# Attention in chunks: pairs of batch entries, each head in a column tile of its own

## The chip, the cores and the metric

One core of a Trainium2 chip runs the whole program. The metric is the device time of one execution in microseconds (us), from the first to the last instruction. TensorE (PE) multiplies matrices; its weight loads stand apart in the profile (PEld). VectorE (DVE), ScalarE (ACT) and GpSimd (POOL) work on elements, and SyncE (SP) issues nearly all DMAs. Matmul results land in PSUM, from where DVE or ACT must move them ("evacuate") to SBUF.

## The reference, cut to what matters

Three stages follow each other. First a recurrence over 768 steps for each of 4 batch entries and 8 heads, with a state of 40x40:

```
for t in range(S):
    y[:, :, t] = einsum('bhd,bhde->bhe', rt, state)
    Sa = einsum('bhde,bhe->bhd', state, at)
    state = state * wt[:, :, None, :] - einsum('bhd,bhe->bhde', Sa, bt)
    state = state + einsum('bhd,bhe->bhde', vt, kt)
```

Its output, as 3072 tokens of 320 values, goes through a mixture of 8 experts (one expert for each token, two layers of 320x1024 and 1024x320), and then through `(a * b) @ w_out` with `a = x @ w_a` and `b = x @ w_b` (1536 wide). The change touches the first stage alone.

## The kernel before, in words

**Chunks.** The recurrence is computed in 12 chunks of 64 steps. Inside a chunk it becomes matrix products: grams of the scaled keys and gates (`gram`), the inverse of a triangular 64x64 matrix (`invert` on DVE and POOL for the 32x32 blocks, `merge` on PE for the block that couples them), then the chain that carries the state, and the outputs. `cum` and `prod` scale the operands, which go to DRAM and come back spread over the partitions (`fetch`, `rfetch`, `spread`).

**Pairs.** Two heads of 64 steps share the 128 partitions: p = 0 in partitions 0 to 63, p = 1 in 64 to 127. A chunk has 16 pairs k, in four groups of four (q = 0 to 3), and the code calls such a group b. Before, a pair is two heads of one batch entry and b is the batch entry.

**The chain of a group** (`chain`, lines 341 to 400) has five parts, C0 to C4. C0 (lines 347 to 358) makes x: for each q one fp16 matmul of `a3` (128 columns of weights, both heads) with the state S of both heads (80 columns), and two float32 matmuls of 64x64 weights with 40 columns, one for each head. The fp16 product gives four blocks of 64x40, of which the two that join a head with its own state are used; so the rows of p = 0 are read at other columns than those of p = 1, and the evacuation is two ACT instructions. C1 (lines 360 to 367) makes u, 64x64 weights and 40 columns, a quadrant of the array for each head. C2 (lines 371 to 385) makes the new state: for each q one fp16 matmul with `sel` (128 columns of weights, 80 streamed) and two float32 matmuls of 128x40 weights, evacuated by two DVE instructions that scale by the decay. C3 and C4 (lines 387 to 399) spread the state over the partitions, and transpose it.

**The outputs of a group** (`outs`, lines 402 to 439): O0 splits and transposes u; O1 makes nf; O2 (lines 422 to 432) makes y: for each q one fp16 matmul of `r3` with the transposed state and one float32 matmul of `nf` (128 columns of weights, both heads) with `z` of both heads (80 columns), evacuated by two DVE instructions. O3 is the gate of the next stage (`gate1`, matmuls at lines 554 and 560).

**float32.** Each float32 matmul of the attention appears in the trace as two loads and two matmuls, that is, two passes: C0 has 16 float32 matmul instructions for its 8 products.

**The order of the work.** `PLAN` (line 479) gives each part of a chunk a place in time, in units of one chunk, and `run` emits the parts sorted by it; the framework then orders the instructions of each engine (line 1038). Each engine takes its queue in order. The preparation of later chunks is emitted between the chains of earlier ones. `warm` (line 336) puts fp16 matmuls of 256 or 512 columns, whose result is overwritten, ahead of most PSUM tiles. The buffers that the change touches: `GT` (scales of y, 3), `QF` (tiles of v and u, 5, one for each group), `Q3`, `P1b`, and `pm`, the PSUM tile of `merge`.

Of the kernel before, what the change touches and what calls it, by code (L numbers as in the profile page):

```python
# [23 lines left out]
def sub(ap, off, dims):  # L24
    """AP on the same tensor: keeps the partition dim of ap, free dims replaced."""
    return bass.AP(tensor=ap.tensor, offset=ap.offset+off, ap=[list(ap.ap[0])]+[list(d) for d in dims])

def host_layout(inp, NC=12):
    f=np.float32
    d={}  # L30
    ct=np.zeros((12,128,5,12,64),f)
    ct[:,:,0]=1.0
    for n,nm in enumerate('wakbr'):
        x=np.asarray(inp[nm]).reshape(4,4,2,12,64,40)       # b q p c t e
        x=x.transpose(3,2,0,1,5,4).reshape(12,2,16,40,64)   # c p k e t
# [15 lines left out]
class Attn:  # L51
    CE=staticmethod(lambda nc: nc.gpsimd)
    PP=(1, 2)
    NP=10      # columns of the inverse (of 16 a partition) that the vector engine computes
    def __init__(s, ctx, tc, ct, vt, x, NC, moe=None):
        s.moe=moe
        s.tc=tc; s.nc=tc.nc; s.ct=ct; s.vt=vt; s.x=x; s.NC=NC
        nc=tc.nc
        mk=lambda n,b,**k: ctx.enter_context(tc.tile_pool(name=n,bufs=b,**k))
        # what is free early lies at the ends, where the next stage's first tiles go  # L60
# [3 lines left out]
        s.ch={}      # per chunk tiles  # L64
# [17 lines left out]
    def setup2(s):  # L82
        nc=s.nc; c=s.c
        z0=c.tile([128,1],F32,name="zz"); nc.gpsimd.memset(z0,0.0)
        s.Z=[c.tile([128,16*104+24],F32,name=f"Z{i}") for i in range(NZ)]     # k p e
        s.TT=[c.tile([128,16,64],F32,name=f"TT{i}") for i in range(2)]
        s.T11=c.tile([128,16,32],F32,name="T11")
        s.P1b=[c.tile([128,4,32],F32,name=f"P1b{i}") for i in range(2)]
        s.DT=[c.tile([128,18],F32,name=f"DT{i}") for i in range(4)]
        s.Q3=[c.tile([128,4,2,128],F16,name=f"Q3{i}") for i in range(QN)]  # L90
# [13 lines left out]
    def scr(s,n,shape,dt,c):  # L104
        """DRAM that is used again: it bounds how far the preparation runs ahead"""
# [4 lines left out]
    def pmt(s,name,n):  # L110
        if n%4==0: s.pm=s.ps.tile([128,512],F32,tag="pm",name=name,bufs=1)
        return s.pm[:,128*(n%4):128*(n%4)+128]
    def tile(s,shape,dt,tag,name,bufs): return (s.pl if tag[:3]=="raw" or tag=="dl" else s.pr if tag in EARLY else s.p2 if tag in MID else s.p3 if tag in LATE else s.p).tile(shape,dt,tag=tag,name=name,bufs=bufs)
    # ---- chunk preparation in the transposed layout
# [5 lines left out]
    def cum(s,c):  # L120
# [63 lines left out]
        # y scale  # L184
# [5 lines left out]
        # decay of the carried state  # L190
# [11 lines left out]
    # ---- spread of the operands over the partitions  # L202
# [35 lines left out]
    # ---- grams and the blocks to invert  # L238
    def gram(s,c):
# [10 lines left out]
        tin=s.dr.tile([2,2,16,32,32],F32,tag="tin",name=f"tin{c}")   # blk p k s t  # L250
# [9 lines left out]
    def invert(s,c):  # L260
# [20 lines left out]
        td=s.dr.tile([2,2,16,32,32],F32,tag="td",name=f"td{c}")     # blk p k s t  # L281
# [11 lines left out]
    def merge(s,c):  # L293
# [3 lines left out]
        for b in range(4):  # L297
            k0=4*b; P1b=s.P1b[b%2]
            pp=s.pmt(f"p1{c}{b}",2*b)
            for q in range(4):  # L300
# [11 lines left out]
            for r in (0,64):  # L312
                nc.scalar.activation(TT[r:r+32,k0:k0+4,32:64],pq[r:r+32,0:128].rearrange("p (q t) -> p q t",q=4),AF.Copy)
# [11 lines left out]
    def vload(s,c):  # L325
        vr=s.tile([128,4,4,40],F32,"vr",f"vr{c}",1)
        s.nc.sync.dma_start(vr.rearrange("p b q e -> p (b q e)"),s.vt[c])
        s.ch.setdefault(c,{})['vr']=vr
    def vsplit(s,c,b):
        nc=s.nc; vr=s.ch[c]['vr'][:,b]  # L330
        Q=s.tile([128,4,2,40],F32,"Q32",f"Qf{c}{b}",QF)
# [3 lines left out]
        s.ch[c][b]=Q  # L335
    def warm(s,ps,k):
        """the array's clock halves when it streams for less than a certain share of the time: columns ahead of the tile's own"""
        n=WARM[k]
        if n: s.nc.tensor.matmul(ps[:,0:n],s.sel[:,4],s.sel[:,0:4].rearrange("p a b -> p (a b)")[:,0:n],start=True,stop=True)
    # ---- one batch entry of one chunk: the chain  # L340
    def chain(s,c,b):
# [4 lines left out]
        s3=lambda t,q: t[0:120,80*q:80*q+80]  # L346
# [18 lines left out]
        for p in (0,1):  # L365
            r=slice(64*p,64*p+64)
            nc.scalar.activation(Q[r,:,p],pu[r,0:160].rearrange("p (q e) -> p q e",q=4),AF.Copy)
        yield
        if c+1<s.NC:
            dt=s.DT[(c+1)%4]  # L370
            pS=s.pst(f"S{c}{b}","pc",2); s.warm(pS,2)
            for q in range(4):
                o=pS[:,q*80:q*80+80]
                if S: mm(o,s.sel[0:120,4],s3(S[0],q),start=True,stop=False)
                n=104*(k0+q)
                if not S: mm(o,z[:,n:n+128],Q[:,q].rearrange("r p e -> r (p e)"),start=True,stop=True)      # 24 columns more are there than used
                else:
# [23 lines left out]
    # ---- one batch entry of one chunk: the outputs  # L401
    def outs(s,c,b):
# [19 lines left out]
        py=s.pst(f"y{c}{b}","po",3); s.warm(py,4)  # L422
        for q in range(4):
# [16 lines left out]
    def step(s,c,b,g,i):  # L440
        """the i-th part of the chain (g=0) or of the outputs (g=1) of one batch entry"""
# [37 lines left out]
PLAN=dict(cum=(18,-3.456,-2.906),prod=(5,-2.906,-2.556),fetch=(3,-2.506,-2.411),gtr=(3,-0.907,-0.897),ztr=(6,-1.79,-1.011),gram=(6,-1.932,-1.922),rfetch=(1,-1.246,-1.236),invert=(64,-1.815,-1.381),tload=(1,-1.122,-1.067),merge=(9,-0.659,-0.209),vpre=(6,-0.796,-0.088),C0=(4,-0.081,-0.071),C1=(4,-0.047,0.086),C2=(4,0.191,0.462),O0=(4,0.315,0.573),C3=(4,0.462,0.734),C4=(4,0.463,0.735),O1=(4,0.586,0.858),O2=(4,0.718,0.96),O3=(2,0.96,1.028))  # L479
# [3 lines left out]
KE=3; CX=8       # blocks that are filled from the first chunks' tokens alone; these chunks  # L483
# [559 lines left out]
```

## Time and profile before

| | |
|---|---|
| median of 3 runs | 1615.24 us |
| the runs | 1615.66, 1615.24, 1597.02 us |
| profiled execution, first to last instruction | 1600.6 us |
| TensorE busy, share of the span | 1331.0 us, 83% |
| VectorE | 897.3 us, 56% |
| ScalarE | 561.6 us, 35% |
| GpSimd | 572.6 us, 36% |
| mean granted TensorE clock, share of the full 2.4 GHz | 0.802 |

The profiled execution has no time beside its span; the span lies between the lowest run and the other two. In the table's shares all three stages are mixed. The matmuls of the first chunk's chain begin around 227 us and the attention's last matmul lies at about 884 us; experts and the last stage follow. A granted clock of 0.50 is 1.2 GHz, one of 1.00 is 2.4 GHz. In a row of a timeline, the first number is the start, the second the time until the modelled end of the last instruction of the row, and "xN" the number of merged instructions; the modelled ends overlap the next row, so durations are read from start to start.

### The profile page before, as it was taken

What the parts mean: (1) busy time and instruction counts of PE and PEld (TensorE: products, weight loads), DVE (VectorE), ACT (ScalarE), POOL (GpSimd) and SP (SyncE); (2) the same over time, 40 slices, a digit from 0 to 9 for tenths busy, and PEclk for the clock granted to TensorE, in tenths of its full rate; (3) what the DMA queues carried; (4) which work ended last, traced back from release to release, by engine and by line L of the source; (5) the groups of instructions that cost most, each with busy time, mean ns of one, the idle gap of its engine ahead of it and who ended that gap; (6) DMA issues with size and microseconds to landing.
All of it is one profiled execution on the core that took longest, in us unless ns stands there. A gap on an engine that the chain in (4) does not pass through costs nothing. (4 is left out here: it accounts for less than half of the span.)

```text
span 1600.6 us, 28092 instructions
## 1 busy us (share of the span) xinstructions
PE 1331.0 (83%) x10765; PEld 1087.4 (68%) x10765; DVE 897.3 (56%) x2192; ACT 561.6 (35%) x1214; POOL 572.6 (36%) x754
## 2 busy tenths in 40 slices
PE   0211279896799999999997989899979999999998
PEld 0111268675577787777886878777856887878787
DVE  9668878566754454454524639998989212121111
ACT  4211345343353443343434224544423223132221
POOL 4535655443442112022115026664445223141221
PEclk9999976555555555555565889998989999999999
DMA  6866655544643323122133126666531101000000
GB/s 207 230 200 188 177 148 155 171 102 136 162 122 96 93 72 96 47 87 65 45 87 95 33 79 192 200 210 183 163 95 62 29 5 33 17 17 18 0 17 17
DMA packets 165284, 166.19 MB, mean 104 GB/s; under 512 B 92213, under 2 KB 130421, under 8 KB 165141
## 3 DMA queue, kind: packets, MB, share of 16 engines
q1 hardware_dynamic: 162741, 156.12, 34.1%
q0 software_dynamic: 2400, 8.20, 1.8%
q8 instruction: 86, 1.41, 0.4%
q14 instruction: 57, 0.47, 0.1%
HBM read 118.43 MB, written 45.84 MB: 103 GB/s over the span
## 5 line engine op out<-in xcount | busy, mean ns | idle before, releaser
L767 POOL TENSOR_TENSOR pL<-pr,pH 128x512 fp32r<-128x512 f32 x72 | 93.0, 1291 | 261.8 <-ACT pH L769 261.7
L786 PE MATMUL ab<-X2H,abh 128*128 128x512 f32 x432 | 172.8, 402 | 1.2 <-ACT sa L977 0.6
L276 DVE TENSOR_TENSOR mA<-tA,tl 128x120 f32<-128x120 f32 (+24 forms) x372 | 115.0, 318 | 83.9 <-DMA tl<-tin 79.3
L978 DVE TENSOR_TENSOR pr<-ab,sa 128x512 f32<-128x512 f32 x72 | 49.6, 689 | 181.4 <-ACT sa L977 181.4
L247 PE MATMUL g<-a,kb 120*128 120x64 f16 x384 | 30.6, 237 | 119.9 <-DMA r<-dr 48.4
L247 PEld LDWEIGHTS <-kb 120*128 120x128 f16 x384 | 25.6, 127 | 153.9 <-issue 132.6
L279 DVE TENSOR_TENSOR tA<-tA,mA 128x120 f32<-128x120 f32 (+24 forms) x372 | 115.2, 320 | 4.8
L426 PE MATMUL y<-Z,nf 128*128 128x80 f32 x384 | 112.6, 449 | 3.6 <-DVE nf L420 3.6
L786 PE MATMUL ab<-X2L,abh 128*128 128x512 f32 x288 | 113.0, 394 | 0.0
L426 PEld LDWEIGHTS y<-Z,nf 128*128 128x128 f32 x384 | 103.5, 333 | 6.6 <-DVE nf L420 3.9
L977 ACT ACTIVATE sa<-ab 128x512 f32<-128x512 f32 x72 | 42.9, 595 | 179.7 <-PE ab L788 179.7
L786 PE MATMUL ph<-XHb,w1h 128*128 128x256 f32 x312 | 93.4, 324 | 6.0 <-DVE hL L855 5.5
L786 PEld LDWEIGHTS ab<-X2H,abh 128*128 128x128 f32 x432 | 81.8, 190 | 21.5 <-issue 2.9
L988 PE MATMUL po<-woh,pH 128*128 128x320 f32 x288 | 93.2, 328 | 3.2 <-ACT woh L932 2.7
L109 POOL TENSOR_TENSOR Q<-Qf,Q 128x320 f16<-128x320 f32 x48 | 39.1, 814 | 154.2 <-ACT Q L407 115.7
L767 POOL TENSOR_TENSOR w1l<-wr,w1h 128x512 fp32r<-128x512 f32 x51 | 70.8, 1404 | 54.2 <-ACT w1h L809 42.0
L786 PE MATMUL ab<-X2H,abl 128*128 128x512 f32 x288 | 89.4, 391 | 0.0
L988 PE MATMUL po<-wol,pH 128*128 128x320 f32 x288 | 88.8, 312 | 0.0
L988 PE MATMUL po<-woh,pL 128*128 128x320 f32 x288 | 88.2, 312 | 0.0
L276 POOL TENSOR_TENSOR mB<-tA,tl 128x18 f32<-128x18 f32 (+7 forms) x121 | 31.0, 256 | 142.8 <-DMA tl<-tin 135.7
L769 ACT ACTIVATE pH<-pr 128x512 fp32r<-128x512 f32 x72 | 45.5, 632 | 100.8 <-DVE pr L978 68.5
L353 PE MATMUL x<-Qf,gm 64*64 64x40 f32 x768 | 77.3, 278 | 0.0
(309 smaller groups left out, 3682.2 us busy)
## 6 DMA issues: line engine op xcount, KB each, us to landing
raw<-ct SPq DMA_DIRECT2D x60, 384.0 KB
kb<-dk SPq DMA_DIRECT2D x36, 360.0 KB
wr<-moe_w SPq DMA_DIRECT2D x40, 320.0 KB
wr<-moe_w SPq DMA_DIRECT2D x40, 256.0 KB
dk<-kb SPq DMA_DIRECT2D x12, 720.0 KB
r<-dr SPq DMA_DIRECT2D x36, 180.0 KB
a<-da SPq DMA_DIRECT2D x36, 180.0 KB
tl<-tin SPq DMA_DIRECT2D x12, 512.0 KB
```

The lines of the kernel that those rows point to most:

```text
L109: def psub(s,out,a,b): s.nc.gpsimd.tensor_tensor(out=out,in0=a,in1=b,op=ALU.subtract)
L247: nc.tensor.matmul(pg[:,(q*2+p)*64:(q*2+p)*64+64], d['kb3'][0:120,k,p], d['a3'][0:120,k,64*p:64*p+64], start=True,stop=True)
L276: E.tensor_tensor(out=t,in0=sub(tA[:,lo,0:1],j,[[32,k],[0,n]]),in1=sub(tl[:,0,0:1],32*j+j+1,[[0,k],[1,n]]),op=ALU.mult)
L279: for E,t,o in ps: E.tensor_tensor(out=o,in0=o,in1=t,op=ALU.add)
L353: mm(px[64*p:64*p+64,q*80+40*p:q*80+40*p+40],gm[r,k0+q,p],Q[r,q,p],start=not S,stop=True)
L426: mm(o,nf[:,2*q:2*q+2].rearrange('p a t -> p (a t)'),sub(z[:,0:1],104*(k0+q),[[64,2],[1,40]]),start=SR is None,stop=True)
L767: def psub(s,L,a,H): s.nc.gpsimd.tensor_tensor(out=L,in0=a,in1=H,op=ALU.subtract)
L769: s.nc.scalar.activation(H,src,AF.Copy)
L786: for i,(a,b) in enumerate(l): mm(o,a,b,start=(i==0),stop=False)
L977: sa=w.tile([128,512],F32,tag="sa",name=f"sa{g}{m}"); nc.scalar.activation(sa,pp[0],AF.Copy)
L978: pr=w.tile([128,512],F32,tag="pr",name=f"pr{g}{m}"); V.tensor_tensor(out=pr,in0=pp[1],in1=sa,op=ALU.mult)
L988: nc.tensor.matmul(po,a[:,m,tk],b[:,m],start=(n==0),stop=(n==35)); n+=1
```

## The change

A pair becomes two batch entries with the same head (the host layout places them so), and a group b is half the heads of two batch entries. Then the products of each head go to the partitions of that head alone (an output at 64p), at columns 40q: each is a matmul of 64 columns of weights with 40 streamed columns, in one of two column tiles of the array, and no cross-head block is computed. In C0 an fp16 matmul with zero weights `zh` clears the PSUM tile, then all `a3` products follow, then all float32 products; in C2 two `sel` products of 160 columns come first, then all `z` products; in O2 each q has two `r3` and two `nf` products. x, the new state and y then lie at the same columns for both p, and one instruction evacuates each. `merge` works on eight pairs at a time in place of four, and the copy of v (`vsplit`) on two groups at a time, with `QF` counting tiles of two groups. `GT` goes from 3 to 2. In `PLAN`, `merge` has 5 parts in place of 9 and `vpre` 4 in place of 6, in the same stretches of time. All other changed lines are comments and docstrings.

```diff
-        x=np.asarray(inp[nm]).reshape(4,4,2,12,64,40)       # b q p c t e
-        x=x.transpose(3,2,0,1,5,4).reshape(12,2,16,40,64)   # c p k e t
+        x=np.asarray(inp[nm]).reshape(2,2,8,12,64,40)
+        x=x.transpose(3,1,0,2,5,4).reshape(12,2,16,40,64)
...
-KB,R3,A3,NZ,GT=1,3,3,4,3
-QN,QF=3,5
+KB,R3,A3,NZ,GT=1,3,3,4,2
+QN,QF=3,3
...
+        s.zh=c.tile([128,128],F16,name="zh"); nc.gpsimd.memset(s.zh,0.0)
...
-        for b in range(4):
-            k0=4*b; P1b=s.P1b[b%2]
+        for b in range(2):
+            k0=8*b; P1b=s.P1b[b%2]
...
-            nc.vector.tensor_scalar(out=Q[r,:,p],in0=vr[r],scalar1=NU,scalar2=None,op0=ALU.mult)
+            nc.vector.tensor_scalar(out=Q[r,:,p].rearrange("r b q e -> r b (q e)"),in0=vr[r,2*f:2*f+2],scalar1=NU,scalar2=None,op0=ALU.mult)
...
-        px=s.pst(f"x{c}{b}","pc",2); s.warm(px,0)
+        px=s.pst(f"x{c}{b}","pc",2)
+        o=lambda t,q,p,n=64: t[64*p:64*p+n,40*q:40*q+40]
+        if S:
+            mm(px[:,0:160],s.zh,s.sel[:,0:2].rearrange("p a b -> p (a b)")[:,0:160],start=True,stop=False)
+            for q in range(4):
+                for p in (0,1):
+                    mm(o(px,q,p),d['a3'][0:120,k0+q,64*p:64*p+64],S[0][0:120,80*q+40*p:80*q+40*p+40],start=False,stop=False)
         for q in range(4):
-            o=px[:,q*80:q*80+80]
-            if S: mm(o,d['a3'][0:120,k0+q],s3(S[0],q),start=True,stop=False)
             for p in (0,1):
                 r=slice(64-64*p,128-64*p)
-                mm(px[64*p:64*p+64,q*80+40*p:q*80+40*p+40],gm[r,k0+q,p],Q[r,q,p],start=not S,stop=True)
+                mm(o(px,q,p),gm[r,k0+q,p],Q[r,p,q],start=not S,stop=not S or q==3)
...
-        for p in (0,1):
-            r=slice(64*p,64*p+64)
-            nc.scalar.activation(X[r],px[r,0:320].rearrange("p (q a e) -> p q a e",q=4,a=2)[:,:,p],AF.Copy,scale=xs)
+        nc.scalar.activation(X,px[:,0:160].rearrange("p (q e) -> p q e",q=4),AF.Copy,scale=xs)
...
+            if S:
+                for p in (0,1):
+                    mm(pS[64*p:64*p+64,0:160],s.sel[0:120,4,64*p:64*p+64],S[0][0:120].rearrange("p (q a e) -> p a q e",q=4,a=2)[:,p],start=True,stop=False)
             for q in range(4):
-                o=pS[:,q*80:q*80+80]
-                if S: mm(o,s.sel[0:120,4],s3(S[0],q),start=True,stop=False)
...
-                    for p in (0,1): mm(o[64*p:64*p+40,40*p:40*p+40],z[:,n+64*p:n+64*p+40],Q[:,q,p],start=False,stop=True)
+                for p in (0,1):
+                    n=104*(k0+q)+64*p
+                    if S: mm(o(pS,q,p,40),z[:,n:n+40],Q[:,p,q],start=False,stop=(q==3))
+                    else: mm(o(pS,q,p),z[:,n:n+64],Q[:,p,q],start=True,stop=True)
...
         for q in range(4):
-            o=py[:,q*80:q*80+80]
-            if SR is not None: mm(o,r3[0:120,k0+q],SR[0:120,q].rearrange("p a e -> p (a e)"),start=True,stop=False)
-            mm(o,nf[:,2*q:2*q+2].rearrange('p a t -> p (a t)'),sub(z[:,0:1],104*(k0+q),[[64,2],[1,40]]),start=SR is None,stop=True)
+            if SR is not None:
+                for p in (0,1): mm(o(py,q,p),r3[0:120,k0+q,64*p:64*p+64],SR[0:120,q,p],start=True,stop=False)
+            for p in (0,1):
+                n=104*(k0+q)+64*p
+                mm(o(py,q,p),nf[:,4*p+q],z[:,n:n+40],start=SR is None,stop=True)
...
-            for p in (0,1):
-                r=slice(64*p,64*p+64)
-                V.tensor_tensor(out=tS[r],in0=pS[r,0:320].rearrange("p (q a e) -> p q a e",q=4,a=2)[:,:,p],in1=sub(dt[r,0:1],k0,[[1,4],[0,40]]),op=ALU.mult)
+            V.tensor_tensor(out=tS,in0=pS[:,0:160].rearrange("p (q e) -> p q e",q=4),in1=sub(dt[:,0:1],k0,[[1,4],[0,40]]),op=ALU.mult)
...
-        for p in (0,1):
-            r=slice(64*p,64*p+64)
-            V.scalar_tensor_tensor(out=y[h,:,p],in0=py[r,0:320].rearrange("p (q a e) -> p q a e",q=4,a=2)[:,:,p],scalar=ys,in1=d['gt'][r,k0:k0+4],op0=ALU.mult,op1=ALU.mult)
+        V.scalar_tensor_tensor(out=y[:,b%2],in0=py[:,0:160].rearrange("p (q e) -> p q e",q=4),scalar=ys,in1=d['gt'][:,k0:k0+4],op0=ALU.mult,op1=ALU.mult)
```

## Rows read from the trace of the kernel before

**Rows 1.** The page: busy time of the engines, and the granted clock in 40 slices.
```profile
PE 1331.0 (83%) x10765; PEld 1087.4 (68%) x10765; DVE 897.3 (56%) x2192; ACT 561.6 (35%) x1214; POOL 572.6 (36%) x754
...
PEclk9999976555555555555565889998989999999999
```

**Rows 2.** Windows: length, busy time (instructions) of PE, PEld, DVE, ACT, POOL; clock; DMA.
```profile
335.00:416.00 81.00, 61.04 (x644) 47.99 (x643) 57.20 (x168) 31.08 (x72) 40.80 (x60) 0.54 0.48 128
...
598.00:656.00 58.00, 54.18 (x603) 43.66 (x600) 26.45 (x98) 23.20 (x63) 11.96 (x33) 0.56 0.26 78
...
227.00:884.00 657.00, 598.25 (x6393) 488.62 (x6391) 351.41 (x1123) 274.36 (x678) 204.09 (x388) 0.56 0.37 102
```

**Rows 3.** Waits of PE, 227 to 884 us: total us, times, longest.
```profile
PE g L247 <- DMA a<-da: 9.9, 3, 3.9
PE y L339 <- DVE nf L420: 8.2, 2, 6.4
```

**Rows 4.** Timeline of PE: n of one group, then y of another.
```profile
561.22 0.61 PE L418 MATMUL n<-r,uv 120*128 120x64 f16 x8
561.64 0.40 PE L339 MATMUL y<-sel 128*128 128x256 f16 x1
561.83 0.27 PE L425 MATMUL y<-SR,r 120*128 120x80 f16 x1
561.90 0.69 PE L426 MATMUL y<-Z,nf 128*128 128x80 f32 x2
...
564.07 0.42 PE L339 MATMUL y<-sel 128*128 128x256 f16 x1
```

**Rows 5.** Timeline of PE: the new state (C2) of one group.
```profile
579.25 0.27 PE L374 MATMUL S<-S,sel 120*128 120x80 f16 x1
579.46 0.36 PE L378 MATMUL S<-Qf,Z 128*40 128x40 f32 x4
579.75 0.25 PE L374 MATMUL S<-S,sel 120*128 120x80 f16 x1
...
581.17 0.39 PE L339 MATMUL S<-sel 128*128 128x256 f16 x1
```

**Rows 6.** Timeline of PE: x (C0) of one group at 1.2 GHz, another at 2.4.
```profile
539.69 0.20 PE L350 MATMUL x<-S,a 120*128 120x80 f16 x1
...
541.22 0.24 PE L321 MATMUL pz<-sel,kb 80*128 80x40 f16 x3
...
544.70 0.26 PE L350 MATMUL x<-S,a 120*128 120x80 f16 x1
544.88 0.44 PE L353 MATMUL x<-Qf,gm 64*64 64x40 f32 x4
545.25 0.25 PE L350 MATMUL x<-S,a 120*128 120x80 f16 x1
...
545.98 0.43 PE L353 MATMUL x<-Qf,gm 64*64 64x40 f32 x2
546.35 0.64 PE L311 MATMUL p<-TT,P1b 32*32 32x32 f32 x16
```

**Rows 7.** Timeline of PE: u (C1) of one group, and the gate's logits.
```profile
575.53 1.08 PE L364 MATMUL u<-X,TT 64*64 64x40 f32 x16
576.54 0.29 PE L411 MATMUL ut<-idh,Q 128*128 128x128 f16 x1
...
577.50 1.53 PE L560 MATMUL lg<-wgt,xt 128*128 128x8 f32 x6
578.96 0.29 PE L411 MATMUL ut<-idh,Q 128*128 128x128 f16 x1
```

**Rows 8.** Lines of the whole span: busy us, mean ns | idle before it.
```profile
L432 DVE SCALAR_TENSOR_TENSOR y<-y,gt 64x160 f32<-64x160 f32 x96 | 30.9, 322 | 74.3 <-PE y L426 73.1
...
L358 ACT ACTIVATE X<-x 64x160 f32<-64x160 f32 x96 | 28.5, 297 | 64.5 <-PE u L364 35.8 <-PE x L353 27.8
```

**Rows 9.** A window at 2.4 GHz, columns as in rows 2.
```profile
595.60:602.40 6.80, 6.80 (x150) 5.75 (x144) 3.36 (x12) 6.39 (x17) 0.00 (x0) 1.00 0.56 163
```

More of the change, by code (lines that the diff above doesn't have):

```diff
@@ L87, in setup2 @@
         s.T11=c.tile([128,16,32],F32,name="T11")
-        s.P1b=[c.tile([128,4,32],F32,name=f"P1b{i}") for i in range(2)]
+        s.P1b=[c.tile([128,8,32],F32,name=f"P1b{i}") for i in range(2)]
         s.DT=[c.tile([128,18],F32,name=f"DT{i}") for i in range(4)]
-        s.Q3=[c.tile([128,4,2,128],F16,name=f"Q3{i}") for i in range(QN)]
+        s.Q3=[c.tile([128,8,128],F16,name=f"Q3{i}") for i in range(QN)]
         s.tH=[c.tile([128,4,128],F16,name=f"tH{i}") for i in range(4)]
@@ L110, in pmt @@
     def pmt(s,name,n):
-        if n%4==0: s.pm=s.ps.tile([128,512],F32,tag="pm",name=name,bufs=1)
-        return s.pm[:,128*(n%4):128*(n%4)+128]
+        if n%2==0: s.pm=s.ps.tile([128,512],F32,tag="pm",name=name,bufs=1)
+        return s.pm[:,256*(n%2):256*(n%2)+256]
     def tile(s,shape,dt,tag,name,bufs): return (s.pl if tag[:3]=="raw" or tag=="dl" else s.pr if tag in EARLY else s.p2 if tag in MID else s.p3 if tag in LATE else s.p).tile(shape,dt,tag=tag,name=name,bufs=bufs)
@@ L296, in merge @@
         yield
-        for b in range(4):
-            k0=4*b; P1b=s.P1b[b%2]
+        for b in range(2):
+            k0=8*b; P1b=s.P1b[b%2]
             pp=s.pmt(f"p1{c}{b}",2*b)
-            for q in range(4):
+            for q in range(8):
                 for p in (0,1):
@@ L304, in merge @@
             for r in (32,96):
-                nc.scalar.activation(P1b[r:r+32],pp[r:r+32,0:128].rearrange("p (q t) -> p q t",q=4),AF.Copy)
+                nc.scalar.activation(P1b[r:r+32],pp[r:r+32].rearrange("p (q t) -> p q t",q=8),AF.Copy)
             yield
             pq=s.pmt(f"t2{c}{b}",2*b+1)
-            for q in range(4):
+            for q in range(8):
                 for p in (0,1):
@@ L325, in vload, with vsplit @@
     def vload(s,c):
-        vr=s.tile([128,4,4,40],F32,"vr",f"vr{c}",1)
-        s.nc.sync.dma_start(vr.rearrange("p b q e -> p (b q e)"),s.vt[c])
+        vr=s.tile([128,4,160],F32,"vr",f"vr{c}",1)
+        s.nc.sync.dma_start(vr.rearrange("p b x -> p (b x)"),s.vt[c])
         s.ch.setdefault(c,{})['vr']=vr
-    def vsplit(s,c,b):
-        nc=s.nc; vr=s.ch[c]['vr'][:,b]
-        Q=s.tile([128,4,2,40],F32,"Q32",f"Qf{c}{b}",QF)
+    def vsplit(s,c,f):
+        nc=s.nc; vr=s.ch[c]['vr']
+        Q=s.tile([128,2,2,4,40],F32,"Q32",f"Qf{c}{f}",QF)
         for p in (0,1):
             r=slice(64-64*p,128-64*p)
-            nc.vector.tensor_scalar(out=Q[r,:,p],in0=vr[r],scalar1=NU,scalar2=None,op0=ALU.mult)
-        s.ch[c][b]=Q
+            nc.vector.tensor_scalar(out=Q[r,:,p].rearrange("r b q e -> r b (q e)"),in0=vr[r,2*f:2*f+2],scalar1=NU,scalar2=None,op0=ALU.mult)
+        for b in (0,1): s.ch[c][2*f+b]=Q[:,b]
     def warm(s,ps,k):
@@ L371, in chain @@
             pS=s.pst(f"S{c}{b}","pc",2); s.warm(pS,2)
+            if S:
+                for p in (0,1):
+                    mm(pS[64*p:64*p+64,0:160],s.sel[0:120,4,64*p:64*p+64],S[0][0:120].rearrange("p (q a e) -> p a q e",q=4,a=2)[:,p],start=True,stop=False)
             for q in range(4):
-                o=pS[:,q*80:q*80+80]
-                if S: mm(o,s.sel[0:120,4],s3(S[0],q),start=True,stop=False)
-                n=104*(k0+q)
-                if not S: mm(o,z[:,n:n+128],Q[:,q].rearrange("r p e -> r (p e)"),start=True,stop=True)
-                else:
-                    for p in (0,1): mm(o[64*p:64*p+40,40*p:40*p+40],z[:,n+64*p:n+64*p+40],Q[:,q,p],start=False,stop=True)
+                for p in (0,1):
+                    n=104*(k0+q)+64*p
+                    if S: mm(o(pS,q,p,40),z[:,n:n+40],Q[:,p,q],start=False,stop=(q==3))
+                    else: mm(o(pS,q,p),z[:,n:n+64],Q[:,p,q],start=True,stop=True)
             tS=s.tile([128,4,40],F32,"tS",f"tS{c}{b}",3)
-            for p in (0,1):
-                r=slice(64*p,64*p+64)
-                V.tensor_tensor(out=tS[r],in0=pS[r,0:320].rearrange("p (q a e) -> p q a e",q=4,a=2)[:,:,p],in1=sub(dt[r,0:1],k0,[[1,4],[0,40]]),op=ALU.mult)
+            V.tensor_tensor(out=tS,in0=pS[:,0:160].rearrange("p (q e) -> p q e",q=4),in1=sub(dt[:,0:1],k0,[[1,4],[0,40]]),op=ALU.mult)
             tH=s.tH[b]
@@ L405, in outs @@
         Qh=s.Q3[s.nu%QN]; s.nu+=1
-        Qv=Q.rearrange("r q p e -> r (q p) e")
-        nc.scalar.activation(sub(Qh[:,0,0,0:1],0,[[128,8],[40,2],[1,40]]),sub(Q[:,0,0,0:1],0,[[40,8],[0,2],[1,40]]),AF.Copy)
-        s.psub(sub(Qh[:,0,0,0:1],80,[[128,8],[1,40]]),Qv,sub(Qh[:,0,0,0:1],0,[[128,8],[1,40]]))
+        Qv=Q.rearrange("r p q e -> r (p q) e")
+        nc.scalar.activation(sub(Qh[:,0,0:1],0,[[128,8],[40,2],[1,40]]),sub(Q[:,0,0,0:1],0,[[40,8],[0,2],[1,40]]),AF.Copy)
+        s.psub(sub(Qh[:,0,0:1],80,[[128,8],[1,40]]),Qv,sub(Qh[:,0,0:1],0,[[128,8],[1,40]]))
         ut=s.ps2.tile([128,8,128],F16,tag="po",name=f"ut{c}{b}",bufs=3)
-        for q in range(4):
-            for p in (0,1): nc.tensor.transpose(ut[:,2*q+p],Qh[:,q,p],s.idh)
+        for a in range(8): nc.tensor.transpose(ut[:,a],Qh[:,a],s.idh)
         uv=s.tile([128,8,128],F16,"uv",f"uv{c}{b}",2)
@@ L417, in outs @@
             for p in (0,1):
-                mm(pn[:,(q*2+p)*64:(q*2+p)*64+64],uv[0:120,2*q+p],r3[0:120,k0+q,64*p:64*p+64],start=True,stop=True)
+                mm(pn[:,(4*p+q)*64:(4*p+q)*64+64],uv[0:120,4*p+q],r3[0:120,k0+q,64*p:64*p+64],start=True,stop=True)
         nf=s.tile([128,8,64],F32,"nf",f"nf{c}{b}",2)
@@ L451, in vpre @@
         yield
-        for b in range(4): s.vsplit(c,b); yield
+        for f in (0,1): s.vsplit(c,f); yield
     def tload(s,c):
@@ L478 @@
 SETUP=(-3.04,-2.3,.05)
-PLAN=dict(cum=(18,-3.456,-2.906),prod=(5,-2.906,-2.556),fetch=(3,-2.506,-2.411),gtr=(3,-0.907,-0.897),ztr=(6,-1.79,-1.011),gram=(6,-1.932,-1.922),rfetch=(1,-1.246,-1.236),invert=(64,-1.815,-1.381),tload=(1,-1.122,-1.067),merge=(9,-0.659,-0.209),vpre=(6,-0.796,-0.088),C0=(4,-0.081,-0.071),C1=(4,-0.047,0.086),C2=(4,0.191,0.462),O0=(4,0.315,0.573),C3=(4,0.462,0.734),C4=(4,0.463,0.735),O1=(4,0.586,0.858),O2=(4,0.718,0.96),O3=(2,0.96,1.028))
+PLAN=dict(cum=(18,-3.456,-2.906),prod=(5,-2.906,-2.556),fetch=(3,-2.506,-2.411),gtr=(3,-0.907,-0.897),ztr=(6,-1.79,-1.011),gram=(6,-1.932,-1.922),rfetch=(1,-1.246,-1.236),invert=(64,-1.815,-1.381),tload=(1,-1.122,-1.067),merge=(5,-0.659,-0.209),vpre=(4,-0.796,-0.088),C0=(4,-0.081,-0.071),C1=(4,-0.047,0.086),C2=(4,0.191,0.462),O0=(4,0.315,0.573),C3=(4,0.462,0.734),C4=(4,0.463,0.735),O1=(4,0.586,0.858),O2=(4,0.718,0.96),O3=(2,0.96,1.028))
 NT=3072; NTI=24; D=320; E=8; F=1024; FF=1536; NB=13; NBT=21
```

16 lines of the change are left out of this document (8 added, 8 removed).

## The prediction

> **What bounds the kernel now.** I read the page first, then windows of the length of a chunk, then PE's waits. The page has PE busy for 83% of the span, and its slices of granted clock fall to 0.5 and 0.6 exactly where the attention runs [rows 1]. From 227 to 884 us, the stretch of all twelve chains, PE is busy for 598.25 of 657 us at a mean clock of 0.56, while DVE has 351, ACT 274 and POOL 204 us [rows 2]. The steady chunk from 598 to 656 has PE at 54.2 of 58 us and no other engine at half. The waits of PE that have a name are small: the largest sum is 9.9 us [rows 3]. So in this stretch the time is what PE needs for its queue at about 1.2 GHz, and an instruction that PE need not stream shortens it. The exception is the chunk from 335 to 416, which took 81 us with PE busy for 61 and DVE for 57 [rows 2]: there the preparation paces PE. Everything after 884 us waits for the attention's tokens and should move with its end.
>
> **The change part by part.** Prices are start to start at 1.2 GHz, for one group (four heads of each p).
>
> *Unit prices.* Eight fp16 matmuls of 64 columns with 128 columns of weights take 561.64 − 561.22 = 0.42 us, 0.053 us each [rows 4]. Six float32 passes with 128 columns of weights and only 8 streamed ones take 1.46 us, so a float32 load of 128 columns costs 0.243 us and one of 64 about 0.122 [rows 7]. The 16 passes of u, 64 columns of weights each, take 1.01 us, 0.063 each [rows 7]: half a load, so two quadrants work side by side and a pair of passes costs 0.126. Where a product of the whole array is followed by one in a tile, 0.18 to 0.21 us pass from start to start [rows 5, 6], although 80 fp16 columns stream in about 0.067 by the unit above: I take 0.12 us for a change of tile shape.
>
> *y (O2).* Four heads of before take 564.07 − 561.83 = 2.24 us, 0.56 each [rows 4], one fp16 matmul and two passes with 128 columns of weights. After, each q has two pairs of float32 passes, 2 × 0.126, and one fp16 pair, 0.053: 0.305. Four of them and two changes of shape: 1.46. Gain 0.78 us, 48 groups.
>
> *The state (C2).* Before 581.17 − 579.25 = 1.92 us [rows 5]. After: one fp16 pair of 160 columns, 0.133 for the stream and 0.053 for a load; then eight pairs of passes. From the four passes of rows 5, 0.29 us with one change of shape, a pair costs (0.29 − 0.12) / 2 = 0.085, so eight take 0.68. With two changes 1.11. Gain 0.81 us, 40 groups.
>
> *x (C0).* Before 545.25 − 544.70 = 0.55 us for each q, 2.2 in all [rows 6]. After: the zeroing matmul 0.133, a change, four fp16 pairs 0.21, a change, then 16 passes as in u, 1.01, which holds the change at its end: 1.59. Gain 0.61 us, 44 groups.
>
> *merge.* The same passes, in four runs for each chunk in place of eight. A run that ends spares two changes of shape when its neighbours use the whole array, so between 0 and 4 × 0.24 = 0.96 us for each chunk; I take the middle, 0.5, 6 us in all.
>
> Sum at 1.2 GHz: 48 × 0.78 + 40 × 0.81 + 44 × 0.61 + 6 = 37 + 32 + 27 + 6 = 102 us. A mean clock of 0.56 means that 12% of the stretch has the full clock, where x of a group takes 541.22 − 539.69 = 1.53 us in place of 2.2 [rows 6]; I take 7% off: 95 us.
>
> *What the rows don't show* is an fp16 product in a column tile, and a column tile that holds all 128 rows beside its neighbour in a long run; the nearest rows are the `z` passes of rows 5. Lower bound of the gain: neighbours' loads in single file. Then a q of y costs 4 × 0.122 + 2 × 0.053 = 0.59, more than the 0.56 of before, and y loses 0.36 us for each group with its two changes; C2 at the 0.073 us for each pass that rows 5 have with the changes inside gains about 0.2, x with eight fp16 products in file about 0.4. Together 9 us of gain. Upper bound: no changes of shape at all and fp16 pairs hidden under loads. Then y takes 1.00, C2 0.81 and x 1.02 us, gains of 1.24, 1.11 and 1.18, which with 7% off make about 150 us. I take the sum above, because the four passes of rows 5 take less than the 4 × 0.076 us that four loads of 40 columns would need in single file plus a change of shape.
>
> [...]
>
> *Evacuations.* One ACT instruction in place of two for x, one DVE instruction in place of two for the state and for y: the ones left out cost 0.30 and 0.32 us [rows 8]. ACT and DVE are at half load in the steady chunk, and both stand waiting for PE ahead of these very instructions (64.5 and 74.3 us in all), so on the path I count 0; without that cover it would be 0.3 us for each, 0.9 us for each group, about 40 us. The larger `merge` and `vsplit` instructions lie on the same half-idle engines and count 0. `GT` = 2 makes the scales of a chunk wait for the y of two chunks earlier; by `PLAN` that y is emitted 0.19 of a chunk sooner, some 10 us, so 0, and what is queued behind it on ACT would wait if that slack went. `QF` still holds more than a chunk. No DMA is added or moved; the memset of `zh` on POOL lies in the setup.
>
> *What reaches the end.* The chunks before 416 us are paced partly by the preparation, whose DVE work does not shrink: a third of the 95 us belongs to them and I keep half of it, −16. In the eight later chunks PE's 4 us of idle time should grow by about 1 us each as it waits more often for the same latencies, −8. That leaves 71 us: 1600.6 − 71 = 1530 us. The profiled execution lies 15 us below the median of the runs and 4 above the lowest, and I give the number on its scale.
>
> **The rivals.**
>
> *The queue's order or the preparation takes half back.* In rows 6, a `merge` run of 32x32 tiles stands in the middle of an x, and could as well cut each grouped run in two: one cut costs 0.24 us, three in each group 32 us at 1.2 GHz. Or the preparation paces five chunks in place of one. For it speaks the chunk of 81 us, against it that DVE and POOL are far from full later. Half of 95 us: 1553, up to 1570 with both.
>
> *The full clock is lost.* The clock reaches 1.00 only in short stretches with PE busy without a gap [rows 9], which is 12% of 657 us, 79 us. The change takes streamed columns away. If none came, the work done there would take 1.4 (x in rows 6) to 2 times as long, 32 to 79 us more: about 1585, no change by measurement. Against it: what shrinks are the long loads, while the streams of `warm` and the transposes stay and stand closer together. By the same argument the full clock may last longer; twice as long would give 55 us, about 1475.
>
> [...]
>
> *Slower: column tiles with all 128 rows in single file*, each load and stream (0.122 + 0.067 us, and 0.053 + 0.033 for fp16) after the other. Place: lines 425 and 426. A q of y would cost 4 × 0.189 + 2 × 0.086 = 0.93, a group 3.95 in place of 2.24, +1.7 us, at 93% over 44 groups +70; C2 gains 6, x 7, `merge` 5: 1653 us. It decides from 0.8 us for each q. Against it: two pairs of passes in rows 5 took 0.29 us, not the 0.57 of single file.
>
> [...]
>
> *The change does not do what it says* is hardly possible for the columns, which the diff fixes; for the grouping it is the first rival.
>
> **How the numbers follow.** Forecast (1495 to 1550) 0.60; half taken back 0.15; full clock lost 0.12; full clock longer 0.07; single file 0.06. The measurement tells about 2% from no change: under 1583 is faster, over 1647 slower. Faster: 0.60 + 0.14 + 0.07 and a little of the lost clock, 0.82; same: the rest of these two, 0.12; slower: 0.06. The range leaves out the single file and the end of the longer clock: 1468 to 1592.
>
> **What would show it.** A group of y near 1.5 us at 1.2 GHz, of the state near 1.1, of x near 1.6; column-tile products of p = 0 and p = 1 starting within some 10 ns of each other; the steady chunk near 49 us; PE still busy for over 85% of it; the clock between 0.54 and 0.62. Wrong would be a y above 2 us, named waits of PE over 5 us in each chunk, or a clock of 0.50 throughout. Equal PE prices and an unmoved end would mean that the preparation was the bound.

## The result, and the profile after

The changed kernel takes 1561.91 us (median of 4 runs, 1557.94 to 1568.07) where the kernel before takes 1611.81 (median of 4). The ratio is 0.9707, 95% interval 0.9657 to 0.9757: faster, by about 47 us. The profiled execution has a span of 1560.7 us (its own time was 1562.75), 40 us less than the span before. 1530 was forecast, in a range of 1468 to 1592.

The page of the changed kernel, busy times and granted clock, which answer to [rows 1]:

```profile
PE 1190.1 (76%) x11497; PEld 974.4 (62%) x11497; DVE 869.3 (56%) x2052; ACT 529.1 (34%) x1070; POOL 572.8 (37%) x755
...
PEclk9999995755765758569566978899999999999999
```

PE lost 141 us of busy time, with 732 instructions more. The span lost 40. So 100 us of what PE saved turned into PE standing still, and the question is for what it stands.

Windows, with the columns of [rows 2], first of the kernel before and then of the changed one. The bounds are three marks that both traces have: x of the first chunk with a carried state, x of the fourth such chunk (the "fourth mark" below), and the last matmul of y. The first mark is the second of the twelve chunks: what the first chunk's chain does lies ahead of 227 us.

```profile
227.00:416.00 189.00, 162.96 (x1728) 131.08 (x1727) 133.79 (x405) 79.26 (x186) 90.80 (x144) 0.56 0.49 135
416.00:879.00 463.00, 430.29 (x4644) 353.01 (x4642) 215.95 (x713) 193.34 (x486) 113.30 (x246) 0.57 0.32 88
879.00:1600.00 721.00, 682.40 (x3672) 561.51 (x3671) 372.86 (x628) 222.10 (x418) 253.22 (x208) 0.96 0.26 76
```

```profile
223.00:404.00 181.00, 125.23 (x1939) 101.88 (x1935) 108.78 (x300) 73.61 (x163) 86.63 (x121) 0.62 0.55 148
404.00:828.00 424.00, 320.19 (x5171) 263.40 (x5165) 211.49 (x676) 171.08 (x390) 117.19 (x267) 0.65 0.36 100
828.00:1560.00 732.00, 691.54 (x3678) 569.07 (x3674) 371.58 (x628) 223.03 (x418) 253.45 (x208) 0.94 0.26 75
```

The attention's later stretch went from 463 to 424 us, −39. The beginning up to the fourth such chunk ends 12 us sooner (404 against 416). What follows the attention takes 11 us longer, at a clock of 0.94 in place of 0.96. In the later stretch PE's idle time went from 33 to 104 us: it is now busy for 76% of it, and no other engine for half. The eight chunks of that stretch take 53 us each, where the prediction had about 49.

The prices of PE, start to start, in stretches with a granted clock of 0.50. One y, with `warm` ahead of it and behind it:

```profile
430.29 0.40 PE L340 MATMUL y<-sel 128*128 128x256 f16 x1
430.62 0.25 PE L427 MATMUL y<-SR,r 120*64 120x40 f16 x2
430.70 0.42 PE L430 MATMUL y<-Z,nf 128*64 128x40 f32 x4
430.92 0.23 PE L427 MATMUL y<-SR,r 120*64 120x40 f16 x2
...
431.89 0.39 PE L340 MATMUL y<-sel 128*128 128x256 f16 x1
```

One new state, then the next product of the whole array:

```profile
566.63 0.42 PE L340 MATMUL S<-sel 128*128 128x256 f16 x1
566.98 0.34 PE L377 MATMUL S<-S,sel 120*64 120x160 f16 x2
567.12 0.74 PE L381 MATMUL S<-Qf,Z 128*40 128x40 f32 x16
567.79 0.61 PE L412 MATMUL ut<-idh,Q 128*128 128x128 f16 x4
```

One x:

```profile
461.35 0.32 PE L351 MATMUL x<-sel,zh 128*128 128x160 f16 x1
461.60 0.40 PE L354 MATMUL x<-S,a 120*64 120x40 f16 x8
461.93 1.08 PE L358 MATMUL x<-Qf,gm 64*64 64x40 f32 x16
462.94 0.32 PE L351 MATMUL x<-sel,zh 128*128 128x160 f16 x1
```

Where `warm` stands ahead, the entry's change of shape is the step from `warm` to the first product less the 0.213 us of its 256 columns (four times the 0.053 us that 64 columns take in [rows 4]): 0.33 − 0.21 for y, 0.35 − 0.21 for the state. So y costs 1.27 + 0.12 = 1.39 us (forecast 1.46; before 2.24 [rows 4]), the state 0.81 + 0.14 = 0.95 (1.11; 1.92 [rows 5]) and x 1.59 (1.59; 2.2 [rows 6]). A q of y takes 0.30 us, 430.92 − 430.62. The groups shown are like the others: the 18 groups of y that ran at a granted clock of 0.50 with nothing between take 1.26 to 1.27 us without the entry, and 19 of the state 0.81. In the groups shown, the products of p = 0 and p = 1 start within 7 ns of each other.

The waits that answer to [rows 3], PE's between 200 and 850 us in the changed kernel:

```profile
PE S L340 <- DVE tS L384: 51.1, 11, 10.8
PE sr L398 <- DVE nf L421: 36.3, 5, 11.4
PE pz L322 <- ACT gt L223: 17.2, 2, 16.7
PE p L304 <- DVE T L296: 12.2, 3, 7.1
```

DVE is at half load, so a want of speed does not explain that it is late. Its own longest wait, before (227 to 884 us) and after:

```profile
DVE mA L276 <- DMA tl<-tin: 57.2, 8, 8.9
```

```profile
DVE mA L277 <- DMA tl<-tin: 96.5, 9, 14.3
```

`mA` is the first instruction of the next chunk's inverse. It waits for `tl`, the blocks of the grams on their way through DRAM. One such wait in the changed kernel, by the timelines of SP, DVE and PE:

```profile
499.48 4.04 SPq L255 DMA_DIRECT2D tin<-gm  x4
...
506.75 0.54 SPq L259 DMA_DIRECT2D tl<-tin  x1
```

```profile
520.10 0.23 DVE L277 TENSOR_TENSOR mA<-tA,tl 128x31 f32<-128x31 f32 x1 [14.32 <-DMA tl<-tin]
...
523.05 0.32 DVE L384 TENSOR_TENSOR tS<-S,DT 128x160 f32<-128x160 f32 x1
```

```profile
511.81 0.47 PE L381 MATMUL S<-Qf,Z 128*40 128x40 f32 x16
512.21 0.45 PE L412 MATMUL ut<-idh,Q 128*128 128x128 f16 x5
523.42 0.37 PE L340 MATMUL S<-sel 128*128 128x256 f16 x1 [10.75 <-DVE tS L384]
```

The state was ready in PSUM soon after 512, but its evacuation stood in DVE's queue behind `mA`, which stood for `tl` from 505.8 to 520.1; PE stood for the evacuation until 523.4. `mA` ran 13 us after the load of `tl` was issued. In the later stretch PE stands for more than 3 us ten times in eight chunks. By the start and end times of the instructions, 49 of PE's 104 idle us there fall into times in which DVE stands for `tl`; in the kernel before it is 4 of 33 us. Not every stop is of this kind: others were for GpSimd's split of the state (11.1 us, once) and for T, which DVE makes when a load of `TT` has landed (10.0 us, twice).

The evacuations, as in [rows 8]:

```profile
L434 DVE SCALAR_TENSOR_TENSOR y<-y,gt 128x160 f32<-128x160 f32 x48 | 15.5, 322 | 29.3 <-PE y L430 26.6 <-PE ptb L840 2.3
...
L361 ACT ACTIVATE X<-x 128x160 f32<-128x160 f32 x48 | 14.6, 303 | 70.9 <-PE u L367 38.0 <-PE x L358 32.4
```

One instruction on 128 partitions takes as long as each of the two halves did, 322 ns and 322 for y, 303 and 297 for x.

### The profile page after: what moved, and what is told of

It reads as the page before. It is cut to its first block, busy times and chain, and to the rows that moved or that the text cites. A ratio compares the mean times of both kernels' runs of the same rounds, so it can differ in the third digit from the quotient of the medians.

```text
span 1560.7 us, 29271 instructions
## 1 busy us (share of the span) xinstructions
PE 1190.1 (76%) x11497; PEld 974.4 (62%) x11497; DVE 869.3 (56%) x2052; ACT 529.1 (34%) x1070; POOL 572.8 (37%) x755
## 5 line engine op out<-in xcount | busy, mean ns | idle before, releaser
L277 DVE TENSOR_TENSOR mA<-tA,tl 128x30 f32<-128x30 f32 (+23 forms) x372 | 124.2, 340 | 120.7 <-DMA tl<-tin 115.3
L280 DVE TENSOR_TENSOR tA<-tA,mA 128x30 f32<-128x30 f32 (+23 forms) x372 | 119.6, 329 | 5.9
L788 PE MATMUL ph<-XHb,w1h 128*128 128x256 f32 x312 | 97.4, 336 | 6.7 <-DVE hL L857 6.2
L788 PEld LDWEIGHTS ph<-XHb,w1h 128*128 128x128 f32 x312 | 65.8, 212 | 19.6 <-DVE hL L857 9.2
L132 DVE TENSOR_TENSOR bf<-bf,raw 128x96 f32<-128x96 f32 x180 | 68.2, 379 | 8.7 <-POOL bf L128 6.6
L340 PE MATMUL S<-sel 128*128 128x256 f16 x88 | 29.7, 337 | 51.8 <-DVE tS L384 51.1
```

Source lines behind the costliest of these rows:

```text
L132: V.tensor_tensor(out=sub(B0,i+1,[[65,24],[46-2*i,2],[16,2]]), in0=sub(B0,i,[[65,24],[48-2*i,2],[16,2]]), in1=sub(W0,i,[[32,24],[15-2*i,2] ...
L277: E.tensor_tensor(out=t,in0=sub(tA[:,lo,0:1],j,[[32,k],[0,n]]),in1=sub(tl[:,0,0:1],32*j+j+1,[[0,k],[1,n]]),op=ALU.mult)
L280: for E,t,o in ps: E.tensor_tensor(out=o,in0=o,in1=t,op=ALU.add)
L788: for i,(a,b) in enumerate(l): mm(o,a,b,start=(i==0),stop=False)
```

## The experiments

Ratios are to the kernel before, run on the same chip; the changed kernel has 0.9707 (0.9657 to 0.9757). Theory 1: the in-order queues, held by the wait for `tl`, hold PE. Theory 2: DMAs and preparation set the pace by themselves. Theory 3: the smaller `GT` and `QF` do. Theory 3 has no run of its own; the trace of the changed kernel speaks against it, since the copy into `gt` waited for a y once, for 1.7 us, and the copies of v waited for their load alone (14.9 us).

**Grams earlier in the plan.**

```diff
-SETUP=(-3.04,-2.3,.05)
+SETUP=(-3.04,-2.5,.05)
-gram=(6,-1.932,-1.922)
+gram=(6,-2.182,-2.172)
```

> The changed kernel with the grams a quarter of a chunk earlier in the plan (and the setup 0.2 of a chunk earlier, which they need). Theory 1 (VectorE's queue is held by the first instruction of the inverse, which waits for the DMA of the grams' blocks, and the evacuations behind it hold TensorE): the wait for tl on VectorE falls from 96 us to under 40, the named waits of TensorE from about 155 us to under 90, and the time from 1562 to 1500-1530. Theory 2 (the DMAs and the preparation themselves are the pace): the wait moves to the grams, which wait for their operands' DMA, or to the merge, and the time stays at 1550-1575. Theory 3 (the smaller buffers of scales and of v hold the queues): no change, 1555-1570.

1551.39 us, 0.9658 (0.9623 to 0.9693): not told apart from the changed kernel. DVE's wait for `tl` did not fall (102.3 us), and GpSimd's rose from 110.8 to 164.0. Theory 1's numbers were missed. The time lies in theory 2's range, and just below theory 3's (inside it by the ratio, 0.9658 × 1611.8 = 1557), so the run does not part these two.

**Inverse later in the plan**, in the changed kernel and in the one before.

```diff
-invert=(64,-1.815,-1.381)
+invert=(64,-1.665,-1.231)
```

> The changed kernel with the inverse 0.15 of a chunk (about 8 us) later in the plan, all else as it is. Theory 1: VectorE's wait for tl falls by about 8 us in each of nine chunks, to 20-40 us, and the time to 1505-1535. Theory 2: the 8 us come back as waits of the merge for the inverse's result, time 1550-1580. Theory 3: 1555-1570.

> The kernel before with the same later inverse. Theory 1 with TensorE as the bound of the kernel before: VectorE's wait for tl (57 us) falls too, but was hidden behind TensorE's queue, so the time stays within 15 us of 1612. If the held queue cost the kernel before as much as the changed one: 1560-1580.

1566.66 us, 0.9758 (0.9727 to 0.9789), with 98.3 us of waiting for `tl` on DVE; and 1607.78 us, 1.0016 (0.9994 to 1.0039). The shift moved next to nothing: in the changed kernel the first `mA` of a chunk keeps its exact place among DVE's instructions in eight of twelve chunks, and moves by 1 to 10 places in the others. The place of an instruction in a queue is the framework's, and `PLAN` alone does not hold it back; that the framework goes by when it expects `tl` is a guess. So these two runs don't test theory 1, and the second says nothing of the kernel before.

**Two evacuations again**, in halves of 64 partitions, for x, the state and y (x shown).

```diff
-        nc.scalar.activation(X,px[:,0:160].rearrange("p (q e) -> p q e",q=4),AF.Copy,scale=xs)
+        for p in (0,1):
+            r=slice(64*p,64*p+64)
+            nc.scalar.activation(X[r],px[r,0:160].rearrange("p (q e) -> p q e",q=4),AF.Copy,scale=xs)
```

> The changed kernel with the evacuations of x, of the state and of y cut in two halves of 64 partitions again. If they count nothing, as forecast: within 8 us of 1562. If one evacuation in place of two is where the gain came from: 1590-1605.

1577.83 us, 0.9809 (0.9752 to 0.9866): between the two numbers. The halves cost about 0.0102 × 1608 = 16 us, by intervals that just touch, so this is hardly clear of noise. In the profiled executions the later stretch is as long as the changed kernel's (423 us, 422 to 845, against 424); the difference lies ahead of the fourth mark, 422 against 404, and why is not shown.

**No wait for `tl`**, in the changed kernel and in the one before: the strongest test, which takes away what the inverse waits for.

```diff
-in1=sub(tl[:,0,0:1],32*j+j+1,[[0,k],[1,n]])
+in1=sub(s.z0,0,[[0,k],[0,n]])
```

> The changed kernel, but the inverse's products on VectorE and GpSimd take a column of zeros in place of the loaded blocks tl, so they wait for no DMA; the loads themselves stay, and the inverse comes out as the identity. Theory 1 (VectorE's in-order queue held by that wait): VectorE's wait for tl is 0, TensorE's named waits in the attention fall from about 155 us to under 80, and the time to 1480-1520. Theory 2 (DMAs and preparation are the pace): the waits move to the merge and the grams, 1545-1570. Theory 3 (smaller buffers): 1550-1570.

> The kernel before with the same zeros. Theory 1: TensorE's own work was the pace there, so the removed wait gives under 20 us, 1585-1610. Theories 2 and 3: 1600-1612. If the wait cost the kernel before as much as the changed one: 1540-1560.

1492.74 us, 0.9277 (0.9214 to 0.9341), and 1531.98 us, 0.9520 (0.9459 to 0.9581). The first is theory 1's number; the second is what theory 1 called impossible, 76 us for the kernel before. In total the change is worth 39 us without the wait, and about 47 with it: this pair of runs does not show that the wait took a part of the change's gain. The windows show where the time went. The kernel before without the wait (first and fourth mark at 175 and 340 us, last y at 806), then the changed one (170, 379, 765):

```profile
175.00:340.00 165.00, 161.07 (x1773) 129.10 (x1772) 107.28 (x341) 78.42 (x189) 75.11 (x116) 0.59 0.57 155
340.00:806.00 466.00, 435.15 (x4686) 353.75 (x4684) 237.58 (x769) 204.96 (x499) 147.33 (x275) 0.57 0.41 112
```

```profile
170.00:379.00 209.00, 137.46 (x1975) 110.65 (x1975) 173.99 (x534) 77.05 (x167) 121.50 (x195) 0.57 0.58 162
379.00:765.00 386.00, 329.05 (x5145) 269.47 (x5140) 166.61 (x473) 171.51 (x391) 107.08 (x196) 0.64 0.42 116
```

In the later stretch the kernel before gains nothing (466 against 463 us): there PE is its pace, as the prediction said. Its whole gain lies ahead of the fourth mark, 340 against 416, and 52 of these 76 us lie ahead of the first mark, 175 against 227, where no chain with a carried state runs. There the changed kernel gains as much (170 against 223). With the zeros DVE begins the first inverse at 9 us in place of 98, so the larger part of what they give the kernel before is that early start, and no held evacuation.

The changed kernel's later stretch is 38 us shorter without the wait (386 against 424), and its beginning, from the first mark to the fourth, is 28 us longer (209 against 181). In part that is work moved from one to the other: DVE runs 534 instructions in this beginning, against 300 with the wait and 341 in the kernel before without it, and 473 in the later stretch, against 676 and 769. So the 80 us between the two later stretches without the wait (466 to 386) can't be set against the 39 with it. From the first mark to the last y the change is worth 36 us without the wait (631 to 595) and 47 with it (652 to 605). What the runs can't part is the wait itself from the inverse's freedom to start early, which zeros give as well.

**The inverse gated by the chain.** A small instruction that reads the state of two chunks earlier must run before the first `mA`, so that `mA` can't stand ahead of that state's evacuation; then the same on GpSimd.

```diff
+        if c>1:
+            g=s.ch[c-2]['gtS']; V.tensor_scalar(out=mA[:,0:1],in0=g,scalar1=0.0,scalar2=None,op0=ALU.mult)
...
+            if b==3: d['gtS']=tS[:,0,0:1]
...
-invert=(64,-1.815,-1.381)
+invert=(64,-1.595,-1.2)
```

> The changed kernel, with the inverse of a chunk emitted after the state of two chunks earlier, and its first VectorE instruction made to depend on that state (one instruction on 128x1), so that the state's evacuation cannot stand behind it. Theory 1: the waits of the state's matmuls for VectorE (51 us) go, those for nf and y stay in part: 1520-1550. Theory 2: the waits move, 1550-1575.

1542.54 us, 0.9588 (0.9521 to 0.9655), in theory 1's range: its interval just ends below that of the changed kernel. DVE's wait for `tl` went from 96.5 to 37.4 us and PE's wait for the state's evacuation from 51.1 to 20.4. But GpSimd's wait for `tl` stood at 120.1, and PE now waited about 35 us each for GpSimd's splits of u and of the state.

```diff
-            g=s.ch[c-2]['gtS']; V.tensor_scalar(out=mA[:,0:1],in0=g,scalar1=0.0,scalar2=None,op0=ALU.mult)
+            g=s.ch[c-2]['gtS']; V.tensor_scalar(out=mA[:,0:1],in0=g,scalar1=0.0,scalar2=None,op0=ALU.mult); s.psub(mB[:,0:1],g,g)
```

> The gate on the state, with GpSimd's share of the inverse gated by one small instruction as well, since GpSimd's queue still waited 120 us for tl in the run with VectorE's gate alone and held the splits of u and of the state. Theory 1 (queues held by the wait for tl, on both engines): GpSimd's wait for tl falls below 60 us and the time to 1510-1535. If only VectorE's queue matters: 1538-1548, as with its gate alone.

1530.14 us, 0.9503 (0.9461 to 0.9545), the fastest kernel here that leaves nothing out: 5.0% below the kernel before and 2% below the changed one. The time is theory 1's; its interval overlaps that of the gate on VectorE alone a little. Between 227 and 839 us:

```profile
DVE mA L279 <- DMA tl<-tin: 51.2, 5, 16.6
```

```profile
POOL mB L279 <- DMA tl<-tin: 65.7, 5, 23.0
```

They are 53% and 59% of the changed kernel's (96.5, and 110.8 on GpSimd); theory 1 had GpSimd's below 60. The profiled execution is one of the longer ones, 1543.21 us, as long as that with VectorE's gate alone (1543.02), so the traces do not show the last 12 us. Its later stretch:

```profile
409.00:817.00 408.00, 313.35 (x5193) 262.31 (x5193) 209.45 (x659) 170.86 (x392) 115.62 (x265) 0.65 0.35 95
```

The stretch is 16 us shorter than the changed kernel's, but PE is still idle for 95 us of it, where it was 104. The waits moved in part, as theory 2 says: PE's largest are now 29.6 us for nf and 20.3 us for GpSimd's split of the state. No run puts the gates into the kernel before, so whether they would help it as much is open.

**Gates at other places.** The inverse gated by nf in place of the state (`invert` at −1.19, `tload` at −0.78, `merge` at −0.5), and both gates with the grams earlier, as in the first run.

> As the last, but the inverse depends on nf of two chunks earlier, 0.6 of a chunk later than now, with the load of its result and the merge moved behind it. Theory 1: VectorE's wait for tl falls below 20 us, the time to 1500-1535 unless the merge comes late for u. Theory 2: the merge waits for the inverse's result, VectorE's wait at L296 over 80 us, 1560-1620.

> Both gates and the grams a quarter of a chunk earlier. Theory 1: the loads have more time before the gate opens, 1500-1530. If the framework's order undoes the plan's times, as the later inverse alone showed: within 10 us of the run with both gates.

1570.95 us, 0.9772 (0.9707 to 0.9837), not told apart from the changed kernel: the wait for `tl` left DVE's list, but the inverse came late for the merge, and PE waited 44.9 us for T. GpSimd, which has no gate in this run, still stood 134.9 us for `tl`, and PE's largest wait, 52.5 us, was for its split of u; the run does not part the two. 1539.93 us, 0.9602 (0.9556 to 0.9649): within 10 us of the run with both gates, as the second expectation had it, but slower, with PE now waiting 28 us for the grams' operands.

**No `warm`.**

```diff
-WARM=(0,256,256,256,256,512,256)
+WARM=(0,0,0,0,0,0,0)
```

> The changed kernel without the fp16 matmuls whose result is overwritten (warm). If the clock carries part of the gain: mean granted clock in the attention falls from 0.65 to 0.50-0.55 and the time rises to 1575-1600. If TensorE's speed no longer sets the pace: 1545-1570, at whatever clock.

1623.19 us, 1.0107 (1.0063 to 1.0151): slower than the kernel before by 1%, and 61 us above the changed kernel, more than either number. Its marks lie at 230, 457 and 895 us:

```profile
230.00:457.00 227.00, 122.36 (x1866) 106.08 (x1866) 118.17 (x317) 73.56 (x162) 87.82 (x130) 0.68 0.46 123
457.00:895.00 438.00, 321.01 (x4966) 278.29 (x4966) 209.01 (x663) 172.06 (x388) 114.61 (x256) 0.55 0.33 91
```

In the later stretch the clock fell to 0.55, as the first theory said, and the stretch is 14 us longer than the changed kernel's, with PE idle for 27% of it. But most of the loss, 53 us, lies ahead of the fourth mark (457 against 404), where PE was busy for 122 us, 3 less than in the changed kernel, and stood idle for 105 of 227 us; the granted clock reads 0.68 there, 0.62 in the changed kernel. So a slower PE does not explain that part, and what does stays open. So the run does not show that the clock is worth 61 us.

**y of the whole array again**, products of 128 columns of weights and 80 streamed, and two evacuations.

```diff
-                for p in (0,1): mm(o(py,q,p),r3[0:120,k0+q,64*p:64*p+64],SR[0:120,q,p],start=True,stop=False)
+            if SR is not None: mm(o,r3[0:120,k0+q],SR[0:120,q].rearrange("p a e -> p (a e)"),start=True,stop=False)
...
```

> The changed kernel with y alone made as before: products of 128 columns of weights and 80 streamed columns, two evacuations. TensorE's price of y at 1.2 GHz returns to 2.2 us a group, 35 us in all. If TensorE is the pace, 1590-1605; if the held queues are, the waits shrink as TensorE gets busier and it is 1565-1582.

1569.14 us, 0.9787 (0.9737 to 0.9837): 13 us more, as for held queues, with intervals that overlap, so it is not told apart from the changed kernel. The later stretch of the profiled execution:

```profile
416.00:840.00 424.00, 335.38 (x4707) 286.59 (x4704) 208.02 (x656) 169.92 (x390) 112.08 (x248) 0.67 0.34 91
```

It is as long as the changed kernel's, with PE busy for 15 us more and idle for 15 us less: there the dearer y fills time in which PE would stand.

## Why the prediction was right, and what in it was not

*Direction, and the number within its range:* right. Of the forecast's 71 us, 40 came in the profiled executions; the measured 1562 lies outside the forecast's own band (1495 to 1550, with 0.60) and in that of the first rival (1553 to 1570), which had 0.15. That it is as near as this is partly luck, since two misses offset each other: in the later stretch PE's busy time fell by 110 us where about 63 were forecast (two thirds of 95), helped by a clock that the sum did not count on, and its idle time grew by 71 us where 8 were forecast.

*The bound.* Right for the later stretch (466 us without and 463 with the wait for `tl`). For the beginning it named one chunk, 335 to 416, as paced by the preparation. The inverse's wait costs the kernel before 24 us between the first mark and the fourth (189 to 165), and 52 us ahead of 227 us, which the prediction did not look at.

*PE's prices.* Right: y 1.39 for 1.46, x 1.59 for 1.59, the state 0.95 for 1.11. Tiles side by side, and no single file: four float32 passes and two fp16 products took 0.30 us where the four loads alone, at the sum's 0.122 each, would need 0.49 in file, and the single-file rival had 0.93. The eight fp16 products of x took 0.33 us with a change of shape, the sum's own 0.21 + 0.12.

*Evacuations.* The step counted 0, with cover on half-idle engines; two in place of one cost 16 us, by intervals that just touch. If that stands, the 0 was wrong, but not in the later stretch, which has the same length with either.

*What reaches the end.* This is the step that failed: "in the eight later chunks PE's 4 us of idle time should grow by about 1 us each". It grew from 33 to 104 us over the stretch, 9 us each. I read the small named waits of PE [rows 3] as a sign that little stood behind PE; but DVE's 57 us of waiting for `tl` was there, hidden because PE had work queued. With PE busy for 110 us less in that stretch, the evacuations behind `mA` became a large part of what PE waits for: 49 of its 104 idle us fall into DVE's waits for `tl`, against 4 of 33 before. The prediction's own sign of being wrong, named waits of PE over 5 us in each chunk, was there too: about 100 us in the eight chunks. A gate that keeps `mA` behind the state's evacuation gained about 19 us, on both engines about 32. The rest is open: with the wait about halved PE still stood for 95 us, for other results, and without it, a kernel whose work lies elsewhere in time, for 57 of 386. The early part, −16 forecast as half kept, came to −12.

*The clock.* The rival that it would be lost is wrong. Its premise does not hold as a count: a q of y streams 240 columns before (80 + 2 × 80) and after (2 × 40 + 4 × 40), now two products at a time. That fewer streamed columns cost clock was the author's estimate; the run nearest to it, without the 256 or 512 columns of each `warm`, has 0.55 where the changed kernel has 0.65. Nor does a clock of 1.00 go with a busy PE throughout: from 227 to 884 us of the kernel before PE stands idle for 3 of the 85 us at 1.00, in the later stretch of the changed kernel for 26 of 131. The one that it stays longer, with 0.07, came true for the clock and not for the time (1475): 0.65 in place of 0.57 in the later stretch, where the granted clock is 0.50 or 1.00, and 1.00 for 131 of 424 us in place of 64 of 463. Its check (0.54 to 0.62) and that of PE's share (over 85%; it was 76%) failed together.

*The end.* "Everything after should move with its end": it grew by 11 us, and why is not shown.

## What to carry to other kernels

Before counting on a shorter bound engine, look through the other engines' in-order queues for long waits that nothing felt so far: a wait for a DMA at the head of a half-idle engine's queue, here of up to 14.3 us, holds the evacuations behind it, and may show only once the bound engine is fast enough to arrive. A plan's due time didn't keep an instruction out of a queue here; a real dependency did, at 19 us of gain on one of the two engines that carry the waiting work and 32 us on both. When such waits were about halved here, PE's idle time only fell from 104 us to 95, with waits for other results in their place, so the idle time of the bound engine is the number to watch, stretch by stretch.

## What the runs showed of the hardware that was not expected

In the later stretch the granted clock rose from 0.57 to 0.65 while PE was busy for less of the time, 76% in place of 93%; without the overwritten fp16 products it was 0.55, with PE busy for 73%. In the first 160 us of the kernel before PE is busy for 27 us, and the granted clock reads 1.00, but the instructions speak against that reading. A `warm` of 512 fp16 columns and the product after it start 0.38 us apart there (85.53 and 85.91 us), as at a reading of 0.50 (392.96 and 393.34), and 0.21 us apart at a reading of 1.00 later (218.41 and 218.62). The trace has no record of the clock before 203 us, and a time without a record reads 1.00; so the first five digits of PEclk in [rows 1] do not show a fast PE. A float32 evacuation of 160 columns took 322 ns on DVE on 64 partitions and on 128 alike, and 297 and 303 ns on ACT.
